# DeltaNet and MLP on one core: another table for the order of all steps

## The chip, the cores and the metric

The kernel runs on one core of a Trainium2 chip. The core has TensorE (PE, with its weight loads shown apart as PEld), VectorE (DVE), ScalarE (ACT), GpSimd (POOL) and SyncE (SP, which only issues transfers). Each engine works through its own queue of instructions in order, and they wait for each other by semaphores. The metric is the time of the whole program on the device, in microseconds (us): the median of several runs.

## The reference, cut to what matters

Two blocks follow each other. The first is a DeltaNet attention: 4 batches, 8 heads, 768 positions, head size 48. Its state is updated position by position:

```
k_n = k / (norm(k) + 1e-06)
for t in range(S):
    y[t]  = q[t] @ state
    v_old = k_n[t] @ state
    state = state + beta[t] * outer(k_n[t], v[t] - v_old)
```

Its output, 4 x 768 rows of 8 x 48 = 384 numbers, is x of the second block, a layer norm and an MLP with 1536 hidden units, all in float32:

```
xn  = (x - mean) / sqrt(var + 1e-06) * g_ln
out = x + max(xn @ w_ch1, 0) @ w_ch2
```

## The kernel before, in words

The 768 positions are cut into 12 chunks of 64. All 32 pairs of batch and head are worked on together, in two groups. A chunk c needs a matrix of products of its keys (G, `gram`), the inverse of a triangular matrix made from it, the masked products of keys and queries (P, `queries`), and then `recur`: products with the state (ks, qs), with the inverse (u), the new state (s), the output (y), and the layer norm. After it block `m<c>` runs the MLP on the 256 rows of the chunk. `fifteen` and `seven` compute the MLP of most chunks with fewer products than usual, by sums and differences of blocks of operands that POOL and DVE make.

The inverse of chunk 0 is found by `first_inverse`: after a first predicated copy, five rounds n = 1 to 5 of doubling, each for both groups: a product E_n on PE (line 774), a predicated copy from it on DVE (line 779), a product Z_n on PE (line 789), and then two readers of Z_n: transposes on DVE (line 738) and three copies back to `xt` on ACT (line 732). The next round's E needs both: the transposes are its operand, and its bank of PSUM must have been read. Group 0 uses bank pair `two`, group 1 `by`. The inverses of the later chunks, x0 (chunk 1), x1 (chunks 2 and 3) and so on, are recurrences in many small DVE steps (`rows_inverse`, lines 910 and 917), fed by loads `gb` of G through DRAM (`gd`).

The weights come as raw words, are fetched on ACT's queue into buffers (`fetch`), and each piece is converted by four steps: two on ACT, one on DVE, one sum on POOL (`convert`, lines 587 to 605). In the first 60 us this runs beside the chain of chunk 0.

All of this is first recorded and not issued: `add` makes a numbered step of every operation (3037 steps, 0 to 3036), with its engine and its predecessors. `emit` then goes through the table `ORDER` and issues the steps in that order. So the table alone sets the order of the work in every engine's queue, the queues of transfers of SP, ACT and POOL among them; `in_this_order` keeps it. The waits follow from the data. [...]

```
if w == "f":
    self.filler[0]()
    continue
...
if s.eng == "Pool" and "bulk" not in s.plan and shared is not seen:
    tc.add_manual_dep(made[n], shared.name, ...)
```

A word `f` in the table issues `zeros` (line 1605): one product of a block of zeros into a part of bank f0 that nothing reads, 128x256. Three other products of zeros, 128x512, are ordinary steps (79, 80 and 81, `fill`, line 620).

The steps by number, as far as they are spoken of:

| steps | what |
|---|---|
| 52 to 59 | loads of k of chunks 0 and 1 (53, 55 on ACT's queue, the others on SP's) |
| 7; 10, 11; 12 to 36 | the block of zeros (DVE); iotas (POOL); masks (DVE) |
| 65, 66; 82 | loads of beta (`brow`) on POOL's queue; PE turns them |
| 8, 9; 41 to 48 | `ident`; copies of the unit matrix (POOL) |
| 85, 86; 105, 106 | PE turns the keys of chunk 0; of chunk 1 |
| 87, 88 | ACT copies the turned keys of chunk 0 |
| 89 to 102 | norms of the keys (ACT, DVE); 92 to 95 end group 0's |
| 103, 104 | G of chunk 0, group 0 and 1 |
| 118, 119, 120 | DVE: scale G, predicated copy, transpose, group 0 |
| 124, 125, 126 | the same of group 1 |
| E_n, group 0 / 1 | 130 / 132, 146 / 148, 162 / 164, 178 / 180, 194 / 196 |
| predicated copies | 131 / 133, 147 / 149, 163 / 165, 179 / 181, 195 / 197 |
| Z_n, group 0 / 1 | 134 / 140, 150 / 156, 166 / 172, 182 / 188, 198 / 202 |
| DVE's transposes of Z1 | 135, 136 / 141, 142 |
| ACT's copies of Z1, Z2, Z3, Z4, group 0 | 137 to 139, 153 to 155, 169 to 171, 185 to 187 |
| ACT's copies of Z5, group 0 | 199 to 201 |
| 206, 207 | P of chunk 0 |
| 215 to 252 | conversions of pieces 0 to 5 of w_ch1 |
| 256 to 263 | loads of `gb` for x0 |
| 310 to 313, 322 to 325 | loads of k of chunks 2 and 3 |
| 316, 317; 318 (G2) | ACT copies the turned keys of chunk 2; its G |
| 334 to 357 | `recur` of chunk 0: 334 first u, 335 its scaling, 338 and 339 y0, 340 copy, 342 to 351 layer norm, 352 transposes, 353 to 355 copies to `xnt` |
| 366, 239 | fetches of weights on ACT's queue |
| 572, 574, ... | first products of m0 |
| 421, 426 | products e1 and z1 of chunk 1's inverse |
| 437, 438; 440, 441; 443; 445 | ks1, qs1; u; s1; y1 of chunk 1 |

Of the kernel before, what the change touches and what calls it, by code (L numbers as in the profile page):

```python
# [131 lines left out]
57 52 54 58-59 56 65-66 10-13 25 14 0 22 28 43 8 44 9 5 7 53 55 79 6 71 77 72 89 37 96 76 97 90 1-2 86 85 80 88 98  # L132
91 105 92 99 15 26-27 23 16 34-35 29-30 17 36 100 93 101 31 19 94 87 103 82 81 104 84 24 83 18 95 102 20-21 118 32
124 74 73 106-107 78 69 38 119 108 219-220 75 39 109 120 33 125 110-111 70 40 f 130-131 126 112 122 128 121 123 f f
f 132 134 400 113 405 64 63 262 257-258 313 411 256 260-261 263 404 410 259 311 68 322 312 403 310 399 324 323 325
67 409 402 408 398 133 136 135 41 45 62 254 225 129 127 231 137 f 140 145 213 138 211 235 139 144 142 141 f f f 146
143 241 245 f f 148 253 47 46 42 659 49-51 147 150 154-155 153 149 156 661 60-61 246 152 157 151 4 f f f 162-163 236
115 114 242 217 243 159 221 160 227 212 161 223 247 264 663 255 48 222 166-168 158 265-266 170-171 169 f f 164 f f
178 215 116 412 229 117 237 224 165 267-268 179 172 182 206-207 270 269 232 184 271-272 183 174 173 664 248 660 208
273 3 274-275 209 226 238 177 175-176 185 210 186-187 f f f 180 314 316 315 194 317 240 244 214 276 181 188 239  # L140
192-193 191 195 277-278 189 279 198 318-319 201 199-200 190 280-281 216 282 228 283 f 196-197 284 334 326 361 367
320 285-288 335 289-292 202 327 338 366 360 293-299 203-204 233 340 342-343 300 328-329 346 205 f f f f 330-331
347-348 671 218 397 230 396 234 352 336-337 339 353 332 354-355 572 574 673 665 662 341 251 249 573 344 575 358-359
250 345 349-350 576 578 406 362 577 579 301 407 321 333 432 431 309 307 302-303 308 304 473 306 305 471-472 474 788
351 356 363 357 252 658 415 433-434 582 580 598 370 364 581 599 373 435 604 583 605 368 584 610 586 365 413 470 414
# [1607 lines left out]
```

## Time and profile before

| what | us |
|---|---|
| three timed runs | 515.43, 519.05, 521.79 |
| their median | 519.05 |
| span of the profiled execution, first to last instruction | 514.1 |
| first matmul starts | 4.37 |
| last matmul ends | 510.33 |
| PE busy | 493.1 |
| DVE busy | 353.5 |
| POOL busy | 284.8 |
| ACT busy | 206.9 |

The profile shows one execution; of its time only the span is given, and the lowest timed run is 1.3 us above that. The page has the busy time of each engine, the span cut into 40 slices of 12.85 us with the busy tenths of each engine, and groups of instructions by line. The trace also answers with busy times by stage and with instructions in order of time; there a line gives the start, the time from the first to the last end of `xN` instructions, engine, line, operation, what is written from what, and in brackets how long the engine sat idle before and what released it. A "busy" PE is not PE at its peak: matmuls are pipelined and their ends are modelled.

### The profile page before, as it was taken

Reading aid. Unit: us, or ns where it says so; the run is one execution under the profiler, and the core shown is the slowest. Engines: PE = TensorE matmul, PEld = TensorE weight load, DVE = VectorE, ACT = ScalarE, POOL = GpSimd, SP = SyncE. Lnnn points to the kernel's source line nnn. Section 1 sums busy time; section 2 is a strip of 40 time slices with the busy share of each in tenths; the row PEclk is TensorE's granted clock in tenths of the full one; section 3 lists DMA queues with packets and bytes.
Section 4 is the critical chain, followed back from the end, with each engine's and each line's share of the span. In section 5 each row is a group of like instructions: output and inputs, shape, how many; then the busy total and the mean of one; then the engine's idle time right before and its main releaser. Section 6 shows DMA issues by size and latency. Waiting matters only on the chain.

```text
span 514.1 us, 22905 instructions
## 1 busy us (share of the span) xinstructions
PE 493.1 (96%) x10022; PEld 450.7 (88%) x10022; DVE 353.5 (69%) x816; ACT 206.9 (40%) x462; POOL 284.8 (55%) x447
## 2 busy tenths in 40 slices
PE   5897899999999999999999999999999999999997
PEld 3675797668888898999999999999999999999996
DVE  4688479899994999975997847898727346254241
ACT  4785764422533333351434343423514425324140
POOL 2634583144658879749477465283274551844644
PEclk9999999999999999999999999999999999999999
DMA  8958895577338755387454474313660321202011
GB/s 207 251 83 192 221 191 127 128 173 117 67 60 207 123 117 92 73 221 123 80 108 62 105 203 76 99 15 53 132 149 12 88 36 41 57 13 82 8 24 31
DMA packets 181635, 54.56 MB, mean 106 GB/s; under 512 B 164888, under 2 KB 177312, under 8 KB 181536
## 3 DMA queue, kind: packets, MB, share of 16 engines
q1 hardware_dynamic: 168512, 40.10, 37.4%
q10 hardware_dynamic: 10816, 9.83, 6.3%
q0 software_dynamic: 2208, 3.17, 4.3%
q8 instruction: 78, 1.28, 1.1%
q14 instruction: 21, 0.17, 0.1%
HBM read 36.30 MB, written 16.78 MB: 103 GB/s over the span
## 4 chain that ended last, share of the span: by engine, by line
PE 85%; DVE 5%; DMA 3%; issue 2%; ACT 1%; SPq 1%; POOL 1%; DVEq 0%; ACTq 0%; POOLq 0%
PE f L1527 28%; PE f L1311 24%; PE f L1430 6%; PE two L822 3%; PE f L1452 3%; DMA tb<-in_q_dram 2%; PE by L1098 2%; PE by L1036 2%; PE two L1091 2%; PE two L1036 2%; PE two L1108 2%; PE f L1605 1%; DVE xb L917 1%; SPq L404 1%; DMA kr<-in_k_dram 1%
## 5 line engine op out<-in xcount | busy, mean ns | idle before, releaser
L1527 PE MATMUL f<-w_sb,h_all 128*128 128x192 f32 x396 | 83.9, 330 | 0.0
L1514 POOL TENSOR_TENSOR h_all<-h_all 128x256 f32<-128x256 f32 x99 | 74.8, 767 | 9.4 <-PE f L1527 3.3
L1527 PE MATMUL f<-words,h_all 128*128 128x192 f32 x396 | 79.5, 329 | 0.2 <-POOL h_all L1514 0.2
L1552 POOL TENSOR_TENSOR words<-h_all 128x128 f32<-128x128 f32 x66 | 30.2, 478 | 74.4 <-ACT h_all L1338 50.2
L1334 DVE TENSOR_TENSOR h_all<-f,h_all 128x512 f32<-128x512 f32 x72 | 49.2, 686 | 30.5 <-PE f L1311 25.9
L1527 PEld LDWEIGHTS f<-w_sb,h_all 128*128 128x128 f32 x396 | 65.3, 190 | 1.6 <-POOL h_all L1514 0.2
L1527 PEld LDWEIGHTS f<-words,h_all 128*128 128x128 f32 x396 | 65.1, 190 | 1.6 <-POOL h_all L1514 1.0
L910 DVE TENSOR_TENSOR tmp<-xb,gb 128x31 f32<-128x31 f32 (+19 forms) x139 | 56.0, 403 | 3.7 <-POOL xb L897 0.5
L917 DVE TENSOR_TENSOR xb<-xb,tmp 128x31 f32<-128x31 f32 (+19 forms) x139 | 51.4, 370 | 2.5
L1329 ACT COPY h_all<-f 128x512 f32<-128x512 f32 x45 | 25.8, 586 | 62.9 <-PE f L1311 39.3
L404 POOL DMA_DIRECT2D tb<-in_k_dram x64 | 41.9, 658 | 8.2 <-PE f L631 7.1
L1338 ACT ACTIVATE h_all<-h_all 128x512 f32<-128x512 f32 x54 | 32.5, 626 | 30.0 <-DVE h_all L1334 29.8
L1311 PE MATMUL f<-x_new,w_sb 128*128 128x128 f32 x288 | 41.4, 278 | 0.0
L1311 PE MATMUL f<-xnt,w_sb 128*128 128x128 f32 x288 | 40.4, 278 | 0.1
L1311 PEld LDWEIGHTS f<-x_new,w_sb 128*128 128x128 f32 x288 | 37.4, 191 | 0.4
L1311 PEld LDWEIGHTS f<-xnt,w_sb 128*128 128x128 f32 x288 | 36.8, 191 | 0.5 <-issue 0.2
L1430 PE MATMUL f<-xnt,w_sb 128*128 128x256 f32 x144 | 33.9, 383 | 0.0
L1430 PEld LDWEIGHTS f<-xnt,w_sb 128*128 128x128 f32 x144 | 26.7, 190 | 3.5
L605 POOL TENSOR_TENSOR w_sb<-words 128x768 uint32<-128x768 uint32 (+1 forms) x11 | 15.3, 1400 | 23.7 <-issue 18.2
L1545 DVE TENSOR_TENSOR o<-f,x 128x192 f32<-128x192 f32 x33 | 11.2, 348 | 24.9 <-PE f L1527 17.2
L1136 ACT COPY x<-by 128x384 f32<-128x384 f32 x23 | 10.6, 481 | 42.6 <-DVE o L1545 27.2
L1527 PE MATMUL f<-w_sb,words 128*128 128x192 f32 x132 | 27.6, 332 | 0.0
(247 smaller groups left out, 1003.6 us busy)
## 6 DMA issues: line engine op xcount, KB each, us to landing
words<-in_moe_w_ch_dram ACTq DMA_DIRECT2D x20, 384.0 KB, 5.2
gd<-gsb SPq DMA_DIRECT2D x11, 512.0 KB, 4.1
v<-in_v_dram SPq DMA_DIRECT2D x24, 192.0 KB, 3.6
kr<-in_k_dram SPq DMA_DIRECT2D x46, 96.0 KB, 3.7
out_dram<-o SPq DMA_DIRECT2D x46, 96.0 KB, 2.5
xld<-xlt SPq DMA_DIRECT2D x9, 384.0 KB, 3.6
xnt<-xld SPq DMA_DIRECT2D x36, 96.0 KB, 3.0
tb<-in_q_dram SPq DMA_DIRECT2D x40, 64.0 KB, 3.5
```

The lines of the kernel that those rows point to most:

```text
L404: add(eng, cost, lambda: QUEUE[eng].dma_start(out=out_, in_=in_), r, w, bulk=n * ns / 16e3, np=n, **kw)
L910: lambda j=j, n=n, w=w, t=t: nc.vector.tensor_tensor(out=t, in0=xv[:, 0:n, j : j + 1].to_broadcast([128, n, w]), in1=gv[:, j : j + 1, j + ...
L917: "DVE", dve(n * w), lambda t=t, rest=rest: nc.vector.tensor_tensor(out=rest, in0=rest, in1=t, op=ALU.subtract),
L1036: nc.tensor.matmul(dst[half(e), hp, j], src[drows(hp), (e if n else key_half(c, hp, e)) * GP + j], s_all[drows(hp), e, j], start=(n == 0 o ...
L1311: nc.tensor.matmul(wide(p[:, f : f + 128]), w[:, f : f + 128], r, start=start and i == 0, stop=True, skip_group_check=True)
L1329: add("ACT", act(512), lambda: nc.scalar.copy(o, p), pk, ok)
L1334: add("DVE", dve(512), lambda: nc.vector.tensor_tensor(out=o, in0=x, in1=y, op=op), [*xk_, *yk], ok)
L1338: add("ACT", act(512), lambda: nc.scalar.activation(o, o, ACTF.Relu, scale=scale), [], ok)
L1430: nc.tensor.matmul(p[:, 0:TOK], w1_sb[:, t, f * 128 : (f + 1) * 128], xnt[:, t], start=(t == 0), stop=(t == KC - 1))
L1514: add(eng, cost, lambda: e.tensor_tensor(out=out_, in0=x, in1=y, op=op), r, w, port=2 if eng == "Pool" else 1, pr=-2)
L1527: lambda f=f, t=start and f == order[0]: nc.tensor.matmul(p[:, 0:D2], lhs(f), rhs[:, f], start=t, stop=(f == order[-1]), skip_group_check=True
L1552: lambda f=f + i: e.tensor_tensor(out=s3[f], in0=one(0, 0)[0](f), in1=one(1, 0)[0](f), op=ALU.subtract),
```

## The change

The text of `ORDER` is replaced. The new table holds the same 3037 steps once each, in another order from the first word to the last. It holds no word `f`; the old one held 25, all ahead of step 572. The rest of the program is the same: `zeros` stays in the code and is not called, and steps 79, 80 and 81 stay. No step is added, taken away or changed, so every engine issues the same instructions as before but for the 25 products and the waits that another order needs. Cut to the opening, up to the first steps of m0, and to the lines around chunk 1's e1, z1, qs1 and s1:

```
 ORDER = """
-57 52 54 58-59 56 65-66 10-13 25 14 0 22 28 43 8 44 9 5 7 53 55 79 6 71 77 72 89 37 96 76 97 90 1-2 86 85 80 88 98
-91 105 92 99 15 26-27 23 16 34-35 29-30 17 36 100 93 101 31 19 94 87 103 82 81 104 84 24 83 18 95 102 20-21 118 32
-124 74 73 106-107 78 69 38 119 108 219-220 75 39 109 120 33 125 110-111 70 40 f 130-131 126 112 122 128 121 123 f f
-f 132 134 400 113 405 64 63 262 257-258 313 411 256 260-261 263 404 410 259 311 68 322 312 403 310 399 324 323 325
-67 409 402 408 398 133 136 135 41 45 62 254 225 129 127 231 137 f 140 145 213 138 211 235 139 144 142 141 f f f 146
-143 241 245 f f 148 253 47 46 42 659 49-51 147 150 154-155 153 149 156 661 60-61 246 152 157 151 4 f f f 162-163 236
-115 114 242 217 243 159 221 160 227 212 161 223 247 264 663 255 48 222 166-168 158 265-266 170-171 169 f f 164 f f
-178 215 116 412 229 117 237 224 165 267-268 179 172 182 206-207 270 269 232 184 271-272 183 174 173 664 248 660 208
-273 3 274-275 209 226 238 177 175-176 185 210 186-187 f f f 180 314 316 315 194 317 240 244 214 276 181 188 239
-192-193 191 195 277-278 189 279 198 318-319 201 199-200 190 280-281 216 282 228 283 f 196-197 284 334 326 361 367
-320 285-288 335 289-292 202 327 338 366 360 293-299 203-204 233 340 342-343 300 328-329 346 205 f f f f 330-331
-347-348 671 218 397 230 396 234 352 336-337 339 353 332 354-355 572 574 673 665 662 341 251 249 573 344 575 358-359
-250 345 349-350 576 578 406 362 577 579 301 407 321 333 432 431 309 307 302-303 308 304 473 306 305 471-472 474 788
...
-606 418 376 603 608 436 666 369 476-479 481-489 480 490-495 375 496-499 670 675 672 1073 674 677 377 371 676 500
-419-420 501 617 607 380 635 609 636 614 391 421 437 502-507 381 508 795 509 439 510-519 424 615 423 612 620 438 384
-390 382 425 422 426 429-430 428 427 637 621 440-441 638 385 392 442 639 445 394 386 447 443 520-523 444 524 393
...
+54 57 59 52 58 56 10-13 5 14-15 17 34 31 66 8 32 1 20 19 22 7 41-42 65 47 62 43 9 48 45 61 55 53 79-80 82 81 6 37-38
+77 39 71 0 86 85 96 89 35 97 90 84 26 23 16 24 72 74 98 73 88 87 99 18 25 27 33 100 83 91 101 28-29 92-94 4 105-106 76
+107-108 104 103 102 95 118 21 124 119-120 125-126 70 40 78 109-111 69 112 122 121 75 123 127-129 113 63 310-311 325
+262 261 256 64 259 257 260 258 263 313 411 312 324 68 67 400 402 410 322 408 323 130 132 131 133 36 134 3 135 30 136
+140 138 137 139 245 143 145 210 225 144 44 49 254 50 659 658 51 60 46 253 661 663 146 142 141 147 150 152 151 148
+154-155 153 219 235 212 243 162 246 149 156 163 166 255 660 157 2 168 158 236 161 159-160 171 169 167 170 237 221 223
+227 264 164 178 165 179 220 224 115 114 182 172 265-269 222 247 117 270 174 184 271-274 215-216 275 183 173 116 187
+177 206-208 176 211 175 185-186 213 180 229 241 248 226 367 238 194 181 314 188 214 662 240 209 195 315 192 191 317
+193 316 239 198 200 189 276-277 190 278-283 242 196 217 366 199 201 318-319 244 334 361 320 284 197 202 326 360 328
+204 203 285-289 335 290-293 327 338 340 294-298 228 299 218 300 329 231 342-343 346-348 233 205 330-331 230 352
+336-337 232 234 664 355 353-354 332 406 409 574 572 339 251 412 301 413-414 470 665 573 249 575 341 344-345 358-359
+578 576 349 579 362 250 350-351 363 407 321 401 403-404 398 303 307 333 405 302 304-305 309 308 306 472 399 432 431
...
+597 602 417 617 595 385 603 376 374 384 635 437 418 600 608 601 606 609 614 380 615 382 607 636 501-502 375 503
+419-420 377 672 1073 673 675 1072 670 674 1075 676 397 677 504-513 439 514-518 381 519-520 795 521 620 421 612 621
+423-425 422 426 390 613 427 429 428 391 430 386 622 637 438 440 638 441 639 442 388 443 522-523 480 524-525 387 526
...
 """
```

196 lines of the change are left out of this document (96 added, 100 removed).

## The prediction

> **What bounds the kernel now.** I read the page's first two parts, then busy time by stage, then the zero products' line, then the timeline of the opening.
>
> The slices show TensorE (PE) full from the fifth slice on, at full granted clock:
>
> ```profile
> PE 493.1 (96%) x10022; PEld 450.7 (88%) x10022; DVE 353.5 (69%) x816; ACT 206.9 (40%) x462; POOL 284.8 (55%) x447
> ...
> PE   5897899999999999999999999999999999999997
> ...
> PEclk9999999999999999999999999999999999999999
> ```
>
> ```profile
> core 0: us, PE busy (x) PEld busy (x) DVE busy (x) ACT busy (x) POOL busy (x), PEclk, DMA share, GB/s
> 0.00:58.00 58.00, 45.08 (x1195) 33.54 (x1195) 37.35 (x127) 38.08 (x89) 25.86 (x45) 1.00 0.82 196
> 58.00:120.00 62.00, 58.79 (x1450) 47.64 (x1443) 50.78 (x116) 29.38 (x68) 27.27 (x30) 1.00 0.68 150
> 120.00:220.00 100.00, 99.38 (x2378) 89.08 (x2377) 88.47 (x184) 36.39 (x91) 73.78 (x100) 1.00 0.56 107
> 220.00:510.00 290.00, 289.48 (x5010) 280.45 (x5009) 176.51 (x390) 103.10 (x215) 157.88 (x274) 1.00 0.36 79
> 510.00:514.10 4.10, 0.33 (x3) 0.03 (x1) 0.36 (x1) 0.00 (x0) 0.00 (x0) 0.82 0.35 96
> ```
>
> At 58.02 the first product of block m0 starts; from there PE is 99% busy. "Busy" hides small stalls, so I measured PE from the start of one step to the start of the next, and took each kind's median as its real need (a half-width product of `seven` 0.325 us, one of `fifteen` 0.447, an attention product of 32 instructions 0.97 to 1.09). From the first matmul (4.37) to the last one's end (510.33) are 506.0 us: 457.4 of need, 6.7 where PE goes from an MLP step to an attention step (71 times 0.095; the new table has 71 too), 15.2 of zero products in the table, 5.3 of the three `fill` steps, 21.4 lost. By stage: before 58.0, 53.6 us hold only **26.6 us of need**; after it 452.3 hold 437.5, so 14.8 are lost (4.4 of them between 80 and 120). So what can be won is the opening, about 27 us, and some of those 14.8.
>
> What sets the opening is no engine's total but a chain over three engines: E_n on PE, a predicated copy on VectorE (DVE), Z_n on PE, then transposes on DVE and copies back on ScalarE (ACT), five rounds, two groups side by side. The 50 records of the 25 zero products (two passes each) lie in just that stretch:
>
> ```profile
> L1605 PE MATMUL f<-u x50: 378/379/483, 15.5 to 53.2; 128*128 128x256 f32 x50
> ```
>
> Here PE after Z1 (first line), and ACT, which must empty bank `two` before E2 may write it:
>
> ```profile
> 19.22 0.65 PE L789 MATMUL two<-xt,gsb 64*64 64x64 f32 x32
> ...
> 23.41 0.69 PE L774 MATMUL two<-qt,gsb 64*64 64x64 f32 x32 [0.78 <-ACT xt L732]
> ```
>
> ```profile
> 20.98 0.37 ACT L732 COPY xt<-two 128x256 f32<-128x256 f32 x1 [0.33 <-DVE qt L738]
> 21.36 0.36 ACT L732 COPY xt<-by 64x256 f32<-64x256 f32 x1
> 21.74 0.20 ACT L677 COPY knat<-knrm 64x8 f32<-64x8 f32 x1
> 21.95 0.37 ACT L732 COPY xt<-two 64x256 f32<-64x256 f32 x1
> 22.34 0.20 ACT L674 COPY knat<-knrm 128x8 f32<-128x8 f32 x1
> 22.44 0.54 ACT L587 ACTIVATE words<-words 128x384 f32<-128x384 f32 x1
> 22.99 0.36 ACT L732 COPY xt<-two 64x256 f32<-64x256 f32 x1
> ```
>
> Z1 ends at 19.87; the three copies need 3 x 0.37 = 1.1 us and end at 23.35, because other work stands between them in ACT's order. E2 starts 0.06 later. That is how this stretch loses time.
>
> **The change, part by part.** *Zero products removed:* 25, 15.2 us of PE. They stand in waits, so I cost them at nothing of their own: with them gone PE sits idle there. Bounds: 0 to 5 us won (the chain of waits gives their line 1%).
>
> *Start.* POOL's two loads of `brow` (1.21 us together) no longer stand ahead of both iotas, so DVE starts near 1.7 instead of 2.90 and builds the masks before about 5, when it was idle from 4.3 to 8.4. Against that, fills 80 and 81 and the beta turn 82 now stand ahead of the first turns 86 and 85, and `ident` (9) and `brow` (65) stand behind copies on POOL that wait for masks. Fill 79 ends near 6.1, 80 near 7.7; 65 is issued near 5.1 and lands 3.2 later (the row of the loads from `beta`), 82 near 8.7, fill 81 (1.06) to 10.1, then 86, 85, 105, 106, 104, 103, six at about 0.62: 13.8. Scaling 118 follows at 13.9, where it was 13.02: **0.9 late**.
>
> *Rounds.* I walked the new queues by hand with the old durations: E 0.69, predicated copy 0.74, Z 0.65, a transpose of half a group 0.43, a copy back 0.37, ACT's conversions 0.55 and 0.9, a hand-off 0.1. After 118, 124, 119, 120, 125, 126 (0.7 each), Z1 of group 0 starts at 19.3 (was 19.22). Now 138, 137, 139 stand together on ACT: 21.15. DVE's 135 and 136 end at 21.5, so E2 starts at 21.6 (was 23.41). In the same way: E3 25.2 (was 29.11), set by ACT's copies 154, 155, 153, which end at 25.05; E4 29.5 (34.37), set by 171, 169, 170 behind four conversions; E5 37.0 (41.43), because nine other ACT steps stand between Z3's copies and Z4's (to 34.4), of which the last, 186, ends at 36.8; c0's first product 334 at 44.5 (48.40), after copies 200, 199, 201 and ACT's steps 316, 239, 217, 366 among them; y0 46.8 (51.00), after DVE's 335; then 340 on ACT, 342 to 348 on DVE to 50.6, transposes 352 to 51.2, ACT's 355, 353, 354 behind 233, 205, 331 to 52.5, and the first product of m0 at **52.6 (58.02)**. Behind what is won, the next late thing is ACT, then the loads of `gb`, landing near 29 by the walk, before ACT asks at 31.6.
>
> The walk gives 5.4 us. It knows no collisions (a subtraction that takes 0.3 us alone took 1.43 at 42.89), so I take **4.5**. Bounds: DVE's work from 131 to 197 is 20.8 us in the new table (21.6 in the old), ACT's from 122 to 200 22.5 (23.1), and the old wall of those stretches is 30.9 and 30.1, so at most about 9; at least -1, the late start alone.
>
> *Moved loads.* SP has kr of chunk 2 and part of chunk 3 ahead of the `gb` loads, where it waited anyway (5.2 to 12.2 and 12.9 to 17.2 idle), and issues the eight `gb` loads nearly in one run instead of spread over 22.2 to 30.1. ACT's weight fetches start about 1 us later. The DMA engines were 93% busy in the first 20 us, so this moves landings both ways; I cost it at nothing, bounds 2 us either way.
>
> *After m0's start.* PE's need is the same. Between e1 and s1 of chunk 1, where most of the 4.4 us were lost (qs1 alone 1.6), the new table puts more m0 products. Against it, PE steps that have under 0.5 us of other PE work between them and the PE step whose result reaches them through other engines rise from 27 to 45 there; 18 x 0.5 us bounds the loss at 9. I take **1.5 won**, bounds -9 to +7 (half of 14.8).
>
> *Sum.* 4.5 + 1.5 = 6.0, on this execution's span of 514.1: 508.1. The three timed runs have 515.43, 519.05 and 521.79, the median 4.95 above that span; carried over, **513.0 us**, 1.2% faster. Two per cent, 10.4 us, is about what this kernel's measurement tells from no change.
>
> [...] The first fill took 2.08 us for two passes, the second 1.02; in the last 4.1 us, with PE done at 510.33, the mean clock is 0.82. So the clock is low at the start and after the end, and nothing between. The longest PE gap of my walk is 1.8 us, before query product 206; gaps of about a microsecond recur in every round.
> [...] No run here shows PE without the zero products.
>
> **Rivals.**
> *Forecast*, 513.0 (509 to 517), 0.47.
> *The stretch reaches its queues' work*: 9 us in the opening and 4 of the 14.8 later, 514.1 - 13 + 4.95 = 506.0. For it: ACT's and DVE's queued work is 9 us under the wall. Against: dependencies leave holes in any order. 0.25.
> *Given back at DVE*: from 80 to 220 DVE is 85 to 95% busy with the recurrences x1, x2, x3 and `differences`; if PE is early and DVE is not, PE waits there. About 5 of the 6 are lost: 518. Against: before 220 the chain of waits is mostly PE's. 0.15. A change that does less than it says belongs here: three fills (5.3 us) stay.
> *The clock falls without the zero products*: PE steps of the opening double, as the two fills show. On the chain lie five E and Z (6.7 us) and as much of turns and products (six of 0.62 at the start, 334, 338, 352, G2): +13.4, and at most the whole 26.6; middle 20, 533. It passes 2% slower from 16.4 us of doubled steps on the chain. Against: from the second fill on, at 7.83, every record is at full clock, a gap of 1.1 us before 9.96 among them. 0.13.
>
> Faster by over 2% is the second case and an edge of the first, 0.26; slower is most of the last, 0.11; within, 0.63. The range 503 to 523 leaves out the last rival and the edge of the second.
>
> **What would show it.** The zero products' line gone; slices 2 to 4 of PE falling to 5 or 6; 118 near 14; E2 before 22.5; m0's first product between 51 and 55; useful PE density after it as before; clock 1.00 throughout. Wrong if E or Z products take over 0.8 us (clock), if m0 starts after 57 (queues), or if PE's share between 80 and 220 falls by 3% or more (DVE).

## The result, and the profile after

The changed kernel takes **539.36 us** (median of 538.02 to 539.79), where the kernel before took 519.12 on the same chip: a ratio of **1.0399** (95% interval 1.0341 to 1.0458; the two medians alone give 1.0390). It is 4% slower. The forecast was 513.0, 1.2% faster, and the range ended at 523.

The profiled execution has a span of 538.0 us, 1.4 below the median. That of before, with 514.1, was the fastest shown. So the two traces differ by 23.9 us, 3.7 more than the medians. The forecast for this span was 508.1.

The page, after, in the same rows: busy time, then PE and the granted clock in 40 slices of 13.45 us.

```profile
PE 496.4 (92%) x9972; PEld 454.5 (84%) x9972; DVE 364.0 (68%) x816; ACT 208.0 (39%) x462; POOL 283.6 (53%) x447
...
PE   6466799899899797999999999999999999999997
...
PEclk9657799899999898999999999999999999999999
```

PE has 50 records fewer, the zero products, and their line is gone. The granted clock, 9 in every slice before, is 5 to 7 in the opening, and three times 8 later; in two of these slices PE has 7. To see where the time went I marked four products in both traces: the first of m0 (step 572, or 574 where that comes first), the first of m1 (826), qs of chunk 5 (1384) and the last (3033).

| us | before | after | more |
|---|---|---|---|
| start to m0 | 58.02 | 64.10 | 6.1 |
| m0 to m1 | 56.1 | 57.2 | 1.1 |
| m1 to qs of chunk 5 | 88.9 | 100.4 | 11.5 |
| qs of chunk 5 to the last product | 306.8 | 312.0 | 5.2 |

The work of PE ahead of each mark, by each kind's own duration, is the same within about 1.5 us, so the stages compare. Busy time by stage, after:

```profile
core 0: us, PE busy (x) PEld busy (x) DVE busy (x) ACT busy (x) POOL busy (x), PEclk, DMA share, GB/s
0.00:64.10 64.10, 40.01 (x1113) 31.93 (x1114) 36.48 (x125) 37.73 (x88) 23.95 (x42) 0.74 0.75 172
64.10:121.30 57.20, 54.89 (x1329) 43.74 (x1325) 43.62 (x104) 29.10 (x68) 25.33 (x28) 0.93 0.66 146
121.30:221.70 100.40, 92.14 (x2113) 80.84 (x2107) 84.87 (x166) 31.11 (x80) 63.54 (x85) 0.97 0.54 104
221.70:534.00 312.30, 309.18 (x5444) 297.98 (x5436) 198.62 (x422) 110.09 (x228) 170.74 (x293) 1.00 0.36 78
```

and the third of these stages in the kernel before:

```profile
core 0: us, PE busy (x) PEld busy (x) DVE busy (x) ACT busy (x) POOL busy (x), PEclk, DMA share, GB/s
114.20:203.00 88.80, 88.38 (x2107) 78.06 (x2105) 77.43 (x167) 32.23 (x84) 63.42 (x85) 1.00 0.60 114
```

For the same instructions within 1% PE is busy 3.8 us longer (the clock, below), DVE 7.4 us more, and PE is idle for 8.3 us where it was idle for 0.4. After's waits of over a microsecond in that stage, in order of time on PE:

```profile
147.82 0.25 PE L979 MATMUL f<-xnj,gsb 32*32 32x32 f32 x3 [1.69 <-issue]
...
180.56 2.51 PE L1425 MATMUL f<-xnt,w_sb 128*128 128x256 f32 x6 [3.56 <-DVE o L1540]
...
211.01 0.59 PE L1522 MATMUL f<-words,h_all 128*128 128x192 f32 x2 [2.77 <-DVE o L1540]
```

The first of these is a stop inside a step, of a kind that comes below ("Waits inside a step"); the other two are waits for DVE. The clock is at half from 181.0 to 184.4 and from 211.7 to 215.2, right behind the two longer waits; 6.8 us at half with PE full are 3.4 us lost. Together 1.69 + 3.56 + 2.77 + 3.4 = 11.4 of the stage's 11.5. What holds DVE there stands in its own order of time:

```profile
172.54 2.97 DVE L1149 TENSOR_SCALAR xln<-x,mv,rstd 128x384 f32<-128x384 f32 x1
175.54 0.58 DVE L1160 STREAM_TRANSPOSE xlt<-xln 128x384 f32<-128x384 f32 x1
176.05 4.20 DVE L1264 SCALAR_TENSOR_TENSOR pt<-w_sb 128x512 f32<-128x512 f32 x1
180.17 0.34 DVE L1540 TENSOR_TENSOR o<-f,o 128x192 f32<-128x192 f32 x1
...
213.00 0.68 DVE L1264 SCALAR_TENSOR_TENSOR qt<-w_more,w_sb 128x512 f32<-128x512 f32 x1
```

The sum in the third line (step 974, a weight sum of `seven`) takes 4.20 us; the last line is the same kind of sum in 0.68. Behind the long one stands 918, the `o` that PE waits for. Beside it POOL runs sums back to back:

```profile
172.57 1.29 POOL L1266 TENSOR_TENSOR w_more<-w_sb 128x512 f32<-128x512 f32 x1
173.80 1.48 POOL L680 TENSOR_TENSOR v<-v,kpair 128x768 f32<-128x768 f32 x1
175.23 0.59 POOL L1547 TENSOR_TENSOR words<-h_all 128x128 f32<-128x128 f32 x1
175.79 1.46 POOL L680 TENSOR_TENSOR v<-v,kpair 128x768 f32<-128x768 f32 x1
177.22 1.25 POOL L1266 TENSOR_TENSOR w_more<-w_sb 128x512 f32<-128x512 f32 x1
178.44 1.25 POOL L1266 TENSOR_TENSOR pt<-w_sb 128x512 f32<-128x512 f32 x1
179.77 1.60 POOL L1266 TENSOR_TENSOR pt<-pt,w_sb 128x512 f32<-128x512 f32 x1
```

Both held steps end beside a POOL step that took longer than its like: `xln` at 175.51 beside a `words` sum of 0.59 (0.46 at 182.56), 974 at 180.25 beside the last line, which needs the line before it and took 1.60 (1.25). In the old table 974 stands elsewhere and takes 0.72. But `xln` (step 955) is held there too, for longer than after. DVE before:

```profile
170.05 3.80 DVE L1154 TENSOR_SCALAR xln<-x,mv,rstd 128x384 f32<-128x384 f32 x1
...
187.03 0.72 DVE L1269 SCALAR_TENSOR_TENSOR pt<-w_sb 128x512 f32<-128x512 f32 x1
```

and POOL beside the first, the end of a run of three sums and two loads:

```profile
172.35 1.27 POOL L1271 TENSOR_TENSOR w_more<-w_more,w_sb 128x512 f32<-128x512 f32 x1
173.57 1.30 POOL L404 DMA_DIRECT2D tb<-in_k_dram  x2
```

All other steps like 955 take 0.44 to 0.67 us in both kernels. So a held step is nothing new; what is new is which steps are held and what stands behind them. Before, 955 and one recurrence step (1125, 2.44 us) are held in this stage, and PE is idle for 0.4 us. After, the longest holds are those of 955, of 974 and of two recurrence steps of x3 (1130 for 2.27 and 1131 for 3.53 us, each 0.4 before), and PE waits for 918 behind 974 and for 1026 behind 1131. Against the shortest time of each step in any of the traces, the DVE steps of this stage take 8.0 us more before and 14.0 after: 6.0 of DVE's 7.4.

### The profile page after: what moved, and what is told of

It reads as the page before. It is cut to its first block, busy times and chain, and to the rows that moved or that the text cites. A ratio compares the mean times of both kernels' runs of the same rounds, so it can differ in the third digit from the quotient of the medians.

```text
span 538.0 us, 22799 instructions
## 1 busy us (share of the span) xinstructions
PE 496.4 (92%) x9972; PEld 454.5 (84%) x9972; DVE 364.0 (68%) x816; ACT 208.0 (39%) x462; POOL 283.6 (53%) x447
## 3 DMA queue, kind: packets, MB, share of 16 engines
q8 instruction: 78, 1.28, 1.0%
## 4 chain that ended last, share of the span: by engine, by line
PE 73%; DVE 11%; DMA 6%; ACT 4%; SPq 3%; issue 2%; ACTq 0%; POOL 0%; DVEq 0%
PE f L1522 23%; PE f L1306 21%; PE f L1425 4%; PE f L1405 3%; PE two L817 3%; PE f L1447 3%; DVE xb L912 3%; DVE tmp L905 3%; SPq L399 3%; PE by L1031 2%; PE by L1093 2%; DMA words<-in_moe_w_ch_dram 2%; PE two L1086 2%; PE two L1103 2%; PE two L1031 1%
## 5 line engine op out<-in xcount | busy, mean ns | idle before, releaser
L1509 POOL TENSOR_TENSOR h_all<-h_all 128x256 f32<-128x256 f32 x99 | 73.1, 751 | 31.5 <-DVE qt L912 9.3
L1522 PE MATMUL f<-w_sb,h_all 128*128 128x192 f32 x396 | 82.0, 332 | 0.3 <-issue 0.3
L1522 PEld LDWEIGHTS f<-words,h_all 128*128 128x128 f32 x396 | 66.3, 194 | 4.4 <-DVE o L1540 3.1
L912 DVE TENSOR_TENSOR xb<-xb,tmp 128x31 f32<-128x31 f32 (+19 forms) x139 | 56.1, 404 | 3.2
L1306 PE MATMUL f<-x_new,w_sb 128*128 128x128 f32 x288 | 39.4, 277 | 0.0
L1425 PE MATMUL f<-xnt,w_sb 128*128 128x256 f32 x144 | 35.4, 393 | 3.6 <-DVE o L1540 3.6
L1306 PEld LDWEIGHTS f<-x_new,w_sb 128*128 128x128 f32 x288 | 36.3, 192 | 0.4
L1540 DVE TENSOR_TENSOR o<-f,x 128x192 f32<-128x192 f32 x33 | 11.5, 351 | 31.6 <-PE f L1522 30.0
L1522 PE MATMUL f<-w_sb,words 128*128 128x192 f32 x132 | 27.8, 333 | 0.7 <-DVE o L1540 0.7
L1131 ACT COPY x<-by 128x384 f32<-128x384 f32 x23 | 10.7, 479 | 41.2 <-POOL o L1540 23.9
```

The lines of the kernel that those rows point to most:

```text
L912: "DVE", dve(n * w), lambda t=t, rest=rest: nc.vector.tensor_tensor(out=rest, in0=rest, in1=t, op=ALU.subtract),
L1306: nc.tensor.matmul(wide(p[:, f : f + 128]), w[:, f : f + 128], r, start=start and i == 0, stop=True, skip_group_check=True)
L1425: nc.tensor.matmul(p[:, 0:TOK], w1_sb[:, t, f * 128 : (f + 1) * 128], xnt[:, t], start=(t == 0), stop=(t == KC - 1))
L1509: add(eng, cost, lambda: e.tensor_tensor(out=out_, in0=x, in1=y, op=op), r, w, port=2 if eng == "Pool" else 1, pr=-2)
L1522: lambda f=f, t=start and f == order[0]: nc.tensor.matmul(p[:, 0:D2], lhs(f), rhs[:, f], start=t, stop=(f == order[-1]), skip_group_check=True
```

## The experiments

All are kernels of one table each, put together from the two tables. Not every wait follows from the data: by `add_manual_dep` in `emit` a POOL step that is not `bulk` waits for the last marked DVE step ahead of it in the table, so these waits go with the order too. "The rest" is what follows a seam in one table, without the steps that stand ahead of it in the other. Ratios are to the kernel before on the same chip, with their 95% interval; the four stage lengths are those of the table above, from one profile each. They differ where the order ahead is the same, too: m0 comes at 61.6 (e1) and 65.4 us (e5), at 62.7 to 64.1 (after, e6, e9, e10, e17), at 60.1 to 61.5 (e2, e8, e13, e14, e15, e18), and from m0 to m1 the same steps took 55.6 (e2), 55.7 (e14) and 59.1 (e13).

### The zero products

The first theory to test was the clock: PE's E and Z products of the opening take 1.13 us after, against 0.69 before. **e1** puts 25 `f` into the new table, ahead of the same PE steps as in the old; **e2** takes them out of the old one.

```
e1:  -... 408 323 130 132 131 ... 186 213 180 ... 233 205 330 ...
     +... 408 323 f 130 f f f 132 131 ... 186 213 f f f 180 ... 233 205 f f f f 330 ...
e2:  -... 70 40 f 130-131 126 112 122 128 121 123 f f f 132 134 ...
     +... 70 40 130-131 126 112 122 128 121 123 132 134 ...
```

> The new table with the 25 zero products put back, ahead of the same next TensorE steps as in the old table. Theory CLOCK (without them TensorE's clock falls to half in the opening, and that makes the chain of chunk 0 late): the granted clock is 1.00 from about 7 us on, m0's first product comes between 52 and 58 us instead of 64.1. Rival QUEUES (the new order of the queues is late even at full clock): it still comes after 62. For the 16 us that the new table loses after m0's start: theory ORDER (the new order behind m0 has its own waits) keeps them, span 524 to 530; rival KNOCK-ON (they follow from the late and slow opening) loses them too, span 508 to 515.

> The old table with its 25 zero products taken out, nothing else. CLOCK: clock at 0.50 for most of 15 to 60 us, m0's first product 5 to 9 us later than 58.0, span 519 to 523. QUEUES: clock may fall, but m0's start stays within 1.5 us of 58 and the span within 512 to 516, since the zero products stood in waits. KNOCK-ON would add more losses behind m0, span 525 or more.

| | us | ratio | to m0 | m0–m1 | m1–qs5 | qs5–last |
|---|---|---|---|---|---|---|
| e1 | 551.07 | 1.0608 (1.0554 to 1.0662) | 61.6 | 67.0 | 99.5 | 316.1 |
| e2 | 519.63 | 1.0011 (0.9983 to 1.0039) | 60.3 | 55.6 | 89.3 | 307.3 |

Without the zeros the clock of the old table falls too. Busy time of e2 in 20 us of the opening:

```profile
core 0: us, PE busy (x) PEld busy (x) DVE busy (x) ACT busy (x) POOL busy (x), PEclk, DMA share, GB/s
20.00:40.00 20.00, 14.55 (x432) 12.88 (x424) 11.15 (x31) 14.69 (x36) 8.64 (x17) 0.52 0.64 97
```

Yet m0 starts only 2.3 us later, and the total doesn't change: the doubled products lie mostly in waits for DVE and ACT. With the zeros the new table runs its opening at nearly full clock (e1: 0.85 from 20 to 30 us, else 0.98 to 1.00). It reaches m0 at 61.6 us in e1 and at 65.4 in e5, which has the same opening, so no gain over the 62.7 to 64.1 without them is shown; and e1 is 12 us slower than the changed kernel. So the zeros keep the clock up, and their absence does not explain the loss. (Most of e1's 12 us are two waits of PE between m0 and m1, 4.14 and 3.42 us, and about 4 us in the last stage; they come back below.)

### Which part of the table

**e3**: the old table until 574, then the rest of the new. **e5**: the new one with `f` until 574, then the old. **e8**: e3 without `f`. Cuts later on: **e13** the old without `f` until 826, then the new; **e14** the same until 1384; **e17** the new until 826, then the old.

```
e3, e8:  old ... 354-355 572 574 | new, rest ... 
e5:      new with f ... 409 574 | old, rest ...
e13:     old without f ... 826 | new, rest ...
e14:     old without f ... 1384 | new, rest ...
e17:     new ... 826 | old without f, rest ...
```

> The old table up to m0's first two products (steps 572 and 574, zero products included), then all other steps in the new table's order. ORDER: m0 starts at 58 as before, and the rest loses about 16 us more than the old rest: span 527 to 532. KNOCK-ON: span 512 to 516.

> The new table up to m0's first product, with the 25 zero products, then all other steps in the old table's order. CLOCK and ORDER together: m0's first product between 52 and 58, nothing lost behind it, span 508 to 514, at or under the kernel before. QUEUES: m0 after 62, span 518 or more.

> The old table without its 25 products of zeros until the first products of m0, then the new one: e3_old_opening_new_rest without its zeros. In e3 (and in e1) TensorE (PE) stood 3.75 us inside step 418, between two products of one step, with nothing it waited for, and then ran at the half clock. Theory FETCH: such stalls come from where in PE's own stream of instructions its blocks are fetched; 25 products fewer shift the blocks, so the gap inside 418 is under 1.5 us, qs1 (438) starts before 97.5 although m0 starts 2 us later than in e3, and the time is 538 to 542 (e3 544.4). Theory ORDER: the gap belongs to what the new order puts at 418; it stays over 3 us, qs1 starts after 99, the time is 545 to 548. Either way it is no faster than the changed kernel by more than 2 us if the new order loses behind m0 by itself, as e3 says.

> The old table without zeros until m1's first product (step 826, 116 us in e2), then the new one. Theory PLACES (behind 826 the loss sits at the held DVE steps near 176 and 205, at the fetch wait near 143 and at z6 and z7, 10 of the 13 us of e8): 527 to 531. Theory EVERYWHERE (the new order has too little cover all along, in proportion to its length): e8's 13.2 us times 400/460, 531 to 533. If the loss is ahead of 826: under 524.

> The old table without zeros until qs5 (step 1384, 205 us in e2), then the new one. PLACES: only the waits at z6 and z7 are left, 520 to 523.5 (e2 519.6). EVERYWHERE: 13.2 times 305/460 on top, 527 to 530.

> The new table until m1's first product (826), then the old one, both without zeros: the other half of e13. If the parts add, e13 and e17 together lose against e2 what the changed kernel loses (19.7 us); with PLACES that is 7 to 11 here, 526.5 to 530.5; with EVERYWHERE, the opening's 5 to 7 and 13.2 times 60/460, 525 to 528, so this run tells the two apart only through the sum.

| | us | ratio | to m0 | m0–m1 | m1–qs5 | qs5–last |
|---|---|---|---|---|---|---|
| e3 | 544.42 | 1.0515 (1.0472 to 1.0558) | 59.6 | 62.0 | 99.7 | 316.8 |
| e5 | 524.59 | 1.0118 (1.0078 to 1.0158) | 65.4 | 57.3 | 89.6 | 306.8 |
| e8 | 532.79 | 1.0290 (1.0231 to 1.0349) | 60.6 | 58.4 | 100.0 | 311.1 |
| e13 | 537.66 | 1.0363 (1.0291 to 1.0434) | 60.3 | 59.1 | 101.6 | 311.8 |
| e14 | 523.23 | 1.0081 (1.0049 to 1.0113) | 60.7 | 55.7 | 89.5 | 310.2 |
| e17 | 525.30 | 1.0131 (1.0072 to 1.0189) | 63.2 | 59.3 | 90.6 | 306.5 |

The stages follow the table that orders them. From m1 to qs of chunk 5 the old order takes 89 to 91 us and the new one 99.5 to 102, whatever stands ahead of it; the last stage 306.5 to 307.6 against 310 to 312, and 315 to 317 in the kernels that carry zeros and the new rest (why, under "Waits inside a step"). e3 and e8 missed their ranges, e3 by being slower than 532 and e8 by being faster than 538. By medians against e2's 519.6 the new order costs 3.6 us from 1384 on (e14), 18.1 from 826 on (e13, more than it was expected to), and 5.7 ahead of 826 (e17). The last two make 23.8, above the 19.7 that the whole change has over e2. Of these 4.1 us about 3.5 lie ahead of e13's seam: up to 826 it issues the same 652 steps in the same order as e2 and e14, and still takes 3.4 to 3.5 us longer from m0 to m1, with a half clock from 98.0 to 101.4 that the other two lack. So the order of those steps is not the cause; scatter of one execution is, or queues that ran ahead of PE into the new part.

### The held DVE steps

The theory: 974 stands ahead of 918 in DVE's queue, is held until POOL's run breaks, and PE waits for 918. **e6** puts 918 ahead of 974, and 1026, the `o` of m2, ahead of the recurrence steps 1131 to 1135 of x3, the first of which was held (all of these are DVE's); **e15** makes the first move alone on e8. The rival: DVE's queue is full whatever the order, and the wait turns up elsewhere.

```
e6, e15:  -... 955 959 974 918 1182 ...
          +... 955 959 918 974 1182 ...
e6 only:  -1129-1130 1131-1132 1106 1133-1135 1373 1375 1377 ... 911 910 961 ...
          +1129-1130 1373 1375 1377 ... 911 910 1026 1131-1132 1106 1133-1135 961 ...
```

> The new table with two steps of VectorE (DVE) put elsewhere in it and nothing else: the sum o<-f,o of m1 (step 918) ahead of the weight sum 974 that took 4.20 us, and o<-f,x of m2 (1026) ahead of the recurrence step 1131 that took 3.53. Theory PORT: DVE is held while GpSimd (POOL) runs its sums one behind the other, and the new table loses behind 160 us because PE's next steps wait for DVE steps that stand behind the held ones. Then PE's idle of 3.56 us at 180.56 and of 2.77 at 211.01 go (under 0.6 each), the half clock at 181 and 211 goes with them, P4 (1192) starts near 180 in place of 184.61, and the time falls by 6 to 9 us, to 530 to 533. Theory SPREAD (the new table is behind because PE has too little other work between dependent steps everywhere; a wait taken away here comes back at the next step): under 3 us of it stay, 536.5 to 540.

> e8_old_opening_no_zeros_new_rest (532.8) with one swap: DVE's sum 918 ahead of the weight sum 974 that POOL's run holds for 4 us. PORT: PE's idle of 3.55 us near 174.6 and the half clock behind it go, and since nothing else is changed 3.5 to 5.5 of it stay: 527 to 529.5. SPREAD (it comes back at the next wait): 531 to 533.

e6: 536.94 us, 1.0352 (1.0291 to 1.0414); stages 62.7, 61.3, 97.3, 310.6. e15: 529.17, 1.0196 (1.0124 to 1.0268), where e8 had 1.0290; stages 61.5, 56.5, 96.2, 310.7. By its time e6 falls into the rival's range. DVE and PE of e15:

```profile
174.37 0.32 DVE L1541 TENSOR_TENSOR o<-f,o 128x192 f32<-128x192 f32 x1
174.61 3.98 DVE L1265 SCALAR_TENSOR_TENSOR pt<-w_sb 128x512 f32<-128x512 f32 x1
```

```profile
173.86 2.75 PE L1426 MATMUL f<-xnt,w_sb 128*128 128x256 f32 x12
176.54 1.15 PE L1032 MATMUL by<-s_all,qt 48*64 48x48 f32 x64
177.51 1.13 PE L818 MATMUL two<-qt,kt 48*64 48x64 f32 x64
```

The sum is held as long as ever (3.98), but nothing waits behind it: PE runs through, and the stage is 3.8 us shorter. The intervals of e15 and e8 overlap, but the wait of 3.55 us that e8 has there is gone from the trace. That settles the first wait. The second did not go but came back, at the P products of chunk 5, in e6:

```profile
214.82 1.16 PE L818 MATMUL two<-qt,kt 48*64 48x64 f32 x64 [3.88 <-DVE qt L798]
```

**e18** puts, on e15, both 1026 and the transposes 1380 that those products need ahead of the same recurrence steps:

```
-1129-1132 1106 1133-1135 1373 ... 910 961 963 965 1374 1201 1199 1378 1376 964 1026 1136 ... 1380 1140
+1129-1130 1373 ... 910 1026 961 963 965 1374 1378 1376 1380 1131-1132 1106 1133-1135 1201 1199 964 1136 ... 1140
```

> e15_old_opening_held_sum_behind (529.2) with DVE's sum 1026 and the transposes 1380 of chunk 5's queries ahead of the recurrence step 1131, in place of behind 1131 to 1139. PORT: PE's idle of 2.64 us at 200.8 (e15) goes and P5 (1381) starts 3 to 6 us earlier than 209.40, with nothing new in its place: 524.5 to 527. If x3, which is put behind, is what PE waits for next: 528 to 530.

529.98 us, 1.0216 (1.0155 to 1.0277): no better than e15, though the stage is 94.4. The wait is 2.21 us now, before another `o` (step 1043):

```profile
207.59 1.24 PE L1523 MATMUL f<-w_sb,words 128*128 128x192 f32 x6 [2.21 <-DVE o L1541]
```

Three orders gave three places for one wait, as the rival says for the second wait. Whether plain work fills DVE there or the steps that are still held (1130 for 2.27 and 1131 for 2.22 us in e18), no run separates.

**e9** tests what lets DVE in: two loads that POOL issues (1551, 1546) are put between its sums.

```
-972 1371 1001 1094 ... 981 980 984 969 975-976 ... 982 1551 1003 1546 1195
+972 1551 1371 1001 1094 ... 981 980 984 1546 969 975-976 ... 982 1003 1195
```

> The new table with two of POOL's loads put between its sums: 1551 behind the first weight sum 972, 1546 ahead of the third, 969. DVE's order is as in the changed kernel, and POOL has the same sums. [...]

546.20 us, 1.0518 (1.0448 to 1.0589); m1–qs5 is 105.4. My estimate, that a load between the sums lets the held step go on and wins 1 to 3 us, missed: neither load (0.65 and 0.68 us) let the held step beside it in, and the longer run held 955 (3.61) and 974 longer.

```profile
179.90 4.89 DVE L1265 SCALAR_TENSOR_TENSOR pt<-w_sb 128x512 f32<-128x512 f32 x1
```

PE's wait for 918 grew with it from 3.56 to 4.90 us, and 17.1 us of this stage ran at half clock instead of 6.8; with PE full that is 5.1 more by estimate, so the clock carries most of e9's 5.0 us. What does end a hold stays open: 955 before ended 0.28 us into the issue of the two loads shown above, and 1131 after 0.35 us into the issue of one. That POOL's sums are what holds DVE is read from the traces, in which the long steps lie beside runs of sums; no run moves the sums away and leaves DVE's order.

### The opening

The prediction's walk let DVE's transposes and ACT's copies read one PSUM bank at the same time. In after they go one by one. ACT of after in round 2:

```profile
21.14 1.16 ACT L727 COPY xt<-two 64x256 f32<-64x256 f32 x3 [3.73 <-DVE qt L733]
22.32 0.90 ACT L582 ACTIVATE words<-words 128x768 f32<-128x768 f32 x1
23.12 0.74 ACT L727 COPY xt<-by 128x256 f32<-128x256 f32 x2
23.89 0.21 ACT L668 ACTIVATE bnat<-ndb 128x16 f32<-128x16 f32 x1
24.01 0.52 ACT L590 ACTIVATE words<-words 128x384 uint32<-128x384 uint32 x1
24.54 0.37 ACT L727 COPY xt<-by 64x256 f32<-64x256 f32 x1
```

and DVE beside it:

```profile
24.94 0.78 DVE L733 STREAM_TRANSPOSE qt<-by 128x256 f32<-128x256 f32 x2 [3.92 <-ACT xt L727]
25.65 0.69 DVE L774 COPY_PREDICATED gsb<-u,two 128x512 f32<-128x512 int32 x1
```

ACT waits 3.73 us for DVE's transposes of `two`, then DVE waits 3.92 us for ACT's copies of `by`, because the table names 143 and 145 ahead of 142 and 141, with conversions between. PE's Z2 waits for the predicated copy behind that:

```profile
22.34 1.13 PE L769 MATMUL two<-qt,gsb 64*64 64x64 f32 x32 [1.15 <-ACT xt L727]
26.39 0.92 PE L784 MATMUL two<-xt,gsb 64*64 64x64 f32 x24 [2.92 <-DVE gsb L774]
```

**e7** lets one engine finish a bank before the other starts, puts E and Z of both groups together, and keeps ACT's conversions behind the copies. **e11** and **e12** are a third opening that also puts the steps of u early and the later fetches late: e11 with 16 `f` (not the 17 of its expectation) and the old rest, e12 without `f`, with the new rest and both moves of e10.

```
e7:        -36 134 3 135 30 136 140 138 137 139 245 143 145 210 225 144 ...
           +36 134 3 135 30 136 140 142 141 138 137 139 143 145 144 245 210 225 ...
e11, e12:  +36 134 140 3 135 30 136 142 141 138 137 139 143 145 144 245 210 225 ...
           +... 198 202 216 200 199 201 217 218 334 335 204 203 205 ... 353-354 248 574 572
```

> The new table with the steps of rounds 1 to 5 (130 to 211) in another order: E and Z of both groups stand together, DVE's transposes of each Z stand directly ahead of ACT's copies of it, and ACT's conversions behind the copies. Theory BANK: the new opening is late because DVE and ACT read the same PSUM bank only one after the other, in the table's order, and the new table lets conversions and the other group's transposes stand between them; then E4 starts near 32.7 (36.73 in the changed kernel), E5 near 38 to 41 (46.43), m0's first product near 60 to 62 (64.10), and the time is 533 to 537. Theory CLOCK: the opening is late because E and Z take 1.1 us at the half clock without the products of zeros; they take that here too, E5 starts after 44 and m0 after 63.5, 537.5 to 540.

> A third order of the opening, then the old table: E and Z of both groups together, DVE's transposes directly ahead of ACT's copies, the scaling of v (214 on POOL) and the turns of q ahead of the weight sums, u, y0 and the layer norm of chunk 0 (334 to 354) ahead of the recurrence x0 and of the weights' later conversions, and 17 products of zeros in waits. Theory BANK (what the opening costs is set by the order of DVE's and ACT's reads and of what stands between them): E5 starts near 38, u (334) near 43 to 45, m0's first product (574) near 50 to 54, where the old table has 58, and most of it stays: 512 to 516. Rival GIVEN BACK: the conversions and x0 that were put behind come due before 100 us, the gain is lost there: 517 to 522.

> The same third opening without zeros, then the new table with the two moves of e10_norm_of_gb_behind. If the parts add (opening 5 to 8 us earlier than the changed kernel's, DVE's held sum 5, norm of gb 1 to 3): m0's first product at 55 to 58, time 522 to 527. If the new rest gives the opening back (DVE or the loads come due at the same time as before): m0 early, but s1 (443) after 101 and the time 529 to 534.

| | E5 of group 0 | first u (334) | m0 | us | ratio |
|---|---|---|---|---|---|
| before | 41.43 | 48.40 | 58.02 | | |
| after | 46.43 | 54.39 | 64.10 | 539.36 | 1.0399 |
| e7 | 41.19 | 54.33 | 63.35 | 540.94 | 1.0435 (1.0374 to 1.0495) |
| e11 | 45.04 | 49.55 | 61.71 | 536.72 | 1.0324 (1.0277 to 1.0370) |
| e12 | 43.79 | 48.21 | 57.72 | 546.67 | 1.0537 (1.0472 to 1.0602) |

(The profiled execution of e11 took 540.98 us, 4.3 over its median.) All three are slower than they were expected to be under any theory. e7 brings E5 back by 5.2 us, at half clock (0.50 from 20 to 30 us, 0.55 from 30 to 40): the order of the rounds is the cause of that loss, the order of the two readers and the conversions between them taken together. But u comes no earlier. POOL's scaling of v, which it needs, stands behind weight sums and ends at 52.35; and in PE's queue product 318 stands ahead of u and waits for ACT until 52.57. In POOL's order of e7:

```profile
47.90 3.03 POOL L601 TENSOR_TENSOR w_sb<-words 128x768 uint32<-128x768 uint32 x3 [1.91 <-DVE tmp L906]
50.88 1.47 POOL L681 TENSOR_TENSOR v<-v,knat 128x768 f32<-128x768 f32 x1
```

With these conversions moved back, e12 reaches m0 at 57.72, and PE then waits for the weights, here in e12:

```profile
72.66 2.50 PE L1405 MATMUL f<-xnt,w_sb 128*128 128x128 f32 x10 [7.77 <-POOL w_sb L600]
```

Its stage from m0 to m1 is 78.5 us; e11 has the same wait, of 9.92. In e11 and e12 E5 is late in another way: E4 comes at 34.43 and 35.13, as early as in e7, but then the query product 206 stands ahead of E5 and waits 3.4 us for ACT. So the opening seems to have two bounds close together, the chain of rounds and the other work on ACT, DVE and POOL; in these three orders, what one won the other gave back.

### Waits inside a step

The two waits between m0 and m1 were left. **e10** moves ACT's norm of chunk 1's `gb` (475), which runs at 79.04 after and at 70.51 before, behind the m0 steps that it delays (with e6's first move); **e19** is e3 with only the first 12 `f`.

```
e10:  -588 587 475 379 589-593 611
      +588 587 379 589-593 475 611
e19:  -f f f 162-163 236 ... 169 f f 164 f f 178 ... 187 f f f 180 ...
      +f f 162-163 236 ... 169 164 178 ... 187 180 ...
```

> The new table with two steps moved: the sum 918 ahead of the weight sum 974 (as in e6_two_sums_behind; 1026 stays where the new table has it), and ACT's norm of gb for chunk 1 (step 475) behind the m0 steps 589, 591 and 593 in place of ahead of them. Theory GB: ACT waits in 475 for the loads of gb, which land at 78 to 80.5 in every kernel with the new order, so whatever the opening wins up to there PE loses at products 590 and 592 (idle 4.24 us in e1, 3.25 in e6, about 1 in the changed kernel). With 475 behind, PE's idle between 74 and 83 is under 0.7 us in sum, m1's first product (826) starts before 121.5, and the time is 530 to 534. Rival: the recurrence x1 that 475 starts is itself late then, and PE waits for chunk 2 between 130 and 160; 535 to 538.

> e3_old_opening_new_rest (544.4) with the first 12 of its 25 products of zeros. FETCH: the gap inside 418 depends on where PE's instruction blocks end, with 48 rows fewer it is under 1.5 us or elsewhere, and the time is 533 to 541. If instead zeros of themselves bring it (by their load on PE or by the earlier start of m0): over 2.5 us inside 418 and 541 to 545.

e10: 540.17 us, 1.0412 (1.0366 to 1.0457); m0–m1 is 64.9. Its expectation missed: the wait for ACT is gone, and one that no engine ended is there, in step 592 (the changed kernel has 0.94 us at this place):

```profile
83.60 4.80 PE L1406 MATMUL f<-xnt,w_sb 128*128 128x128 f32 x27 [3.10 <-issue]
```

e19: 540.66 us, 1.0408 (1.0345 to 1.0471); 58.0, 58.8, 99.7, 315.1. First e3, with 25 zeros, then e19, with 12:

```profile
81.67 1.22 PE L949 MATMUL by<-xt,es 32*32 32x32 f32 x112
86.64 0.44 PE L949 MATMUL by<-xt,es 32*32 32x32 f32 x16 [3.75 <-issue]
```

```profile
72.66 5.74 PE L1406 MATMUL f<-xnt,w_sb 128*128 128x128 f32 x49 [1.58 <-issue]
...
85.07 1.72 PE L1406 MATMUL f<-xnt,w_sb 128*128 128x128 f32 x14 [2.36 <-issue]
```

In e3 PE stops for 3.75 us in the midst of step 418, between two of its 128 equal records (64 products of two passes), where the kernel has no wait. Each such stop ends shortly behind a 16-KB packet of the queue that carries instructions (q8, 78 packets, 1.28 MB): in e3 that packet lies at 84.16 to 85.29, in e19 packets at 69.60 to 71.20 and 82.45 to 83.65. The traces of all kernels have 44 stops of over 0.8 us inside a step behind 62 us, and all end 1.2 to 1.9 us after the end of such a packet, where 12% of arbitrary times would. With other numbers of PE instructions ahead the stops move to other steps; without zeros the longest in step 418 is 0.82 us (e13). The reading that fits is that PE ran out of instructions there. Why a packet came late is open: the DMA engines were busy for 88% of the time from 80 to 84 us in e3 and for all of it in e10, but no run changed that alone.

These stops are most of what the zeros cost with the new rest. e3 differs from e8 by the 25 `f` alone and is 7.9 us longer by the profiles: behind m0, waits of over 0.8 us that no engine ended make 8.5 us in e3, 4.0 of them in the last stage, and 2.6 in e8, none of them there. Before has one such stop, of 1.26 us, and after three with 3.5 us in sum.

## Why the prediction was wrong, point by point

*Zero products at nothing: right for the time, but not for its reason.* e2 changes the time by 0.1%. The prediction held the clock at full without the zeros, which no run had shown; it fell (to 0.52 from 20 to 40 us in e2), and the doubled steps then lay in waits. The mechanism of the rival "the clock falls without the zero products" was real, and its price wrong: it gave 20 us of doubled steps on the chain, and 27.8 us at half clock ahead of m0, 20.5 of them in a row, moved m0 by 2.3 in e2. The test "E or Z over 0.8 us" fired (1.13) and named a cause that holds little of the loss. *The gaps of PE.* The walk's longest was 1.8 us, and the clock was put at full beside it. It fell with no PE idle longer than 1.99 us (after) and 1.51 us (e2) ahead of the first fall.

*Start: 1.2 us better than forecast.* Step 118 started at 12.68, 0.3 earlier than before, where the walk had 13.9, 0.9 later. E2 came at 22.34, before the 22.5 given, but by luck: from 118 to E2 the walk has 7.7 us and the trace 9.7.

*Rounds: the step that failed in the opening.* By the walk E3, E4, E5, u and m0 come at 25.2, 29.5, 37.0, 44.5 and 52.6; they came at 29.69, 36.73, 46.43, 54.39 and 64.10. The walk was 0.7 us out at E2 and 4.5 one round later, where ACT and DVE go one by one through the banks, with conversions between (e7). "It knows no collisions" was priced at 0.9 us. Of the 10.6 us between the 4.5 won and the 6.1 lost at m0, the zeros explain about 2 at most (the old opening reaches m0 at 58.0 and 59.6 with them, at 60.1 to 61.5 without; for the new one no such gain shows). 5.2 at E5 are the order of the rounds (e7); that POOL's sums ahead of v and PE's product 318 then take their place is what e7's trace shows. The rest is not taken apart. "m0 after 57 (queues)" was the test that named it.

*Moved loads at nothing: no wait for them in after, over 2 us in kernels that share its order.* The `gb` loads of chunk 1 were issued at 72.2 to 74.5 instead of 61.6 to 64.7, and ACT asked for them ahead of m0's hidden blocks. In e6, e17 and e1 PE waited 3.3 to 4.1 us for that; after has no such wait, as ACT's step came late enough without it.

*After m0's start, 1.5 won, bounds −9 to +7: the largest error.* It is 17.8 us lost: 1.1 to m1, 11.5 to qs of chunk 5, 5.2 behind. The prediction counted PE steps with little PE work between them. The loss came instead from what stands behind what on DVE, with POOL's sums beside it. "Given back at DVE" had the right engine and the right stretch (PE busy from 80 to 220 fell from 136.84 to 129.44 us, 5.4%, where 3% was the test), but priced it at 5 us, as a queue that is full; it did not see that the new order makes other DVE steps longer (974 took 4.20 for 0.72, 1131 took 3.53 for 0.41), that PE's next steps stand behind these, and that the half clock comes behind PE's waits (3.56 and 2.77 us; 3.41 us at half from 181.0 and from 211.7). The old trace had the sign of it, 955 with 3.80 for 0.48. Of the 11.5 us, only the wait behind 974 is shown by a run that takes it away (e15, 3.8 us of a stage); the other is argued. In the last stage PE is idle for 2.4 of the 5.2 us more, nearly all in three waits (0.72 for DVE's `o`, 0.77 and 0.96 for ACT's `es`), and busy for 2.8 longer with the same steps at full clock; no run takes these apart.

*Two readings that change no term.* PE's slices before are full from the sixth on, the fifth has 8. DVE's share between 80 and 220, by 20 us, runs from 73% to 97%, and not from 85 to 95.

*Sum.* On the profiled span 508.1 was predicted and 538.0 measured: 29.9 us, of which 10.6 are the opening and 19.3 what follows. The carry-over added 4.95; after needed 1.4.

## What to carry to other kernels

A new order keeps every instruction, but not every duration (974 took 0.72 us before, 4.20 after): before moving work, look in the old trace for an engine's steps that take several times their usual time (here 955, 3.80 for 0.48), see which engine runs without a break beside them, and keep whatever the bounding engine needs out of the queue behind them. When a chain passes through two engines that read the same bank, walk it as one after the other, in table order (in after ACT waited 3.73 us for DVE's reads of `two`, then DVE 3.92 for ACT's of `by`). And test a wait by moving only the step that stands behind it: if the wait comes back at another place, more than that one step is late, and moving it alone does not help.

## What was not expected of the hardware

- A DVE step beside back-to-back POOL sums was held through several of them, before as after: 3.80 (before), 2.97, 4.20 and 3.53 (after), 3.98 (e15) and 4.89 us (e9) for steps of 0.4 to 0.7. Some holds ended beside a sum that took longer than its like (after: 0.59 for 0.46, 1.60 for 1.25), others in the issue of a load (0.28 us into it before, 0.35 after); in e9 an issue between the sums ended none. After's 974, from 176.05 to 180.25, did not wait for one sum alone: beside it POOL ran most of a sum of 1.46 us, two of 1.25 and the start of one of 1.60.
- In after the half clock came in six stretches of 23.89, 6.83, 6.83 and three times 3.41 us, that is 7, 2, 2, 1, 1 and 1 times 3.41: the first two from 17.2 to 41.1 and from 44.5 to 51.3. Two of 3.41 stand right behind single waits of 3.56 and 2.77 us late in the kernel; with PE full each costs 1.7 us on top of the wait, by estimate (half of 3.41). Length alone does not tell: a stop of 1.70 us brought one in e15 (at 144.56), one of 1.69 none in after (at 147.82).
- 25 products of 128x256, 15.2 us of PE, held the clock at full through the old opening (before, e3) and mostly so in the new (e1 and e5: at half for 3.4 and 10.2 us ahead of m0, where after has 33.3). With the first 12 of them it stayed full to 40 us in the old opening and fell later (e19: 0.84, then 0.72 from 50 to 58); m0 came at 57.97, where none gave 60.62 (e8) and 25 gave 59.56 (e3). For the start of m0, then, the clock decides little.
- A stream of products can, by the reading above, run ahead of its instructions: stops of up to 3.75 us inside a step, each ending 1.2 to 1.9 us behind a packet of instructions. They move with the number of instructions ahead, so that a few products more or less at the start shift them to other places 30 us later.
